# Scratch of the weight sums in a pool of its own, and the pools of the sums opened at once

## Chip, core and metric

The kernel runs on one core of one Trainium2 chip. The metric is the device time of one execution in microseconds (us), the median of several runs. The engines are TensorE (PE, its weight loads as PEld), VectorE (DVE), ScalarE (ACT), GpSimd (POOL) and SyncE (SP, which here only issues transfers). Each engine takes its instructions in the order of its own list and stops at the first one whose inputs are not there.

## What is computed

Sliding-window attention with eight global keys, then a two-layer network with a leaky ReLU. Four sequences of 768 positions, 8 heads of 64, give 3072 tokens of 512 numbers; the hidden width is 2048. The weights come as float64 and everything is to be right in float32, so each factor of the network is split into a high and a low part and each product takes three matmuls.

```python
scores = scale * np.matmul(q, k.transpose(0, 1, 3, 2))
keep = is_global | is_local
scores = np.where(keep, scores + bias, -1e9)
a = np.exp(scores - scores.max(-1, keepdims=True))
x = np.matmul(a / (a.sum(-1, keepdims=True) + 1e-09), v)   # per head, then tokens x 512
h = x @ w_in                                               # 512 -> 2048
return np.maximum(0.01 * h, h) @ w_out                     # 2048 -> 512
```

## The kernel before

Attention is cut into 48 units (24 blocks of 128 tokens, two halves of the heads). The work of unit t is spread over three events: event t forms its scores on PE, adds the bias and takes the row minimum on DVE (L224), takes the exponentials on ACT (L237), and scales them by the reciprocal of their sum (L258, L259, then L268 on DVE or L266 on ACT). From unit 14 on the probabilities `pr` are turned on DVE in blocks of 32 (L283) and sent by SP through memory, out as `via` (L248) and back as `pt_d` in four transfers (L250). Event t+2 multiplies them with the values (`attn_v`, L351) and ACT copies the result `x` (L357).

The network goes over the tokens in chunks: two chunks of three blocks, then nine of two. The first two chunks (the middle stage) work with one sixteenth of the hidden width at a time (`ffn1`, `ffn2`, helper lines L990 to L1012), beside the conversion of the weights. Its last outputs are held in three tiles `kept` of the pool `ev` and added to by DVE (L452). The nine chunks of the last stage work in 72 steps s, eight per chunk. Step s has one pair p of hidden blocks:

- `hidden_pair(s)`: 24 matmuls (L496) into one PSUM bank, `ps_h` for even s, `ps_p` for odd s.
- `gates(s)`: ACT copies the bank (L507), DVE applies the leaky ReLU (L509) and, where the pair is done with seven products in place of eight, four sums of its blocks (L512), ACT rounds to the high part `gh` (L516), DVE takes the rest `gl` (L518).
- `out_pair(s - 2)`: 12 matmuls with eight products, 21 with seven, over `gh` and `gl` (L548), two steps later.

So `gates` has two steps of PE time before its result is needed. Seven products stand in for eight because sums of blocks of the output weights `wout` are formed once, pair by pair. This is the work of `prepare(p, part)`: four parts for a pair, each three additions on DVE into two scratch tiles `wk` (L528), one rounding on ACT into `h` (L665) and one subtraction on DVE into `l` (L528); part 3 writes back into `wout`. In what follows, each such DVE instruction is called a sum instruction. The parts are handed to `gates` by the table `sums_at`: two parts a step at s = 2 to 7 (pairs 7, 6, 5, 4), then one a step at s = 8 to 23 (pair 3, the last part of pairs 7 to 4, then pairs 2 and 1).

The scratch tiles come from the pool `ev`, which has three buffers. The same three buffers hold `kept` before, and the output rows `part` and the tile `u` of `results` (L627) at the end of each chunk, from where SP sends them out (L460, L647). A tile that takes a buffer over waits until its last user is done, a transfer among them.

At s = 0 the pools of the middle stage are closed (`later`) and the pools `a` (gh, gl) and `w` (the sums h, l) are opened in their room.

PE's instructions are in the order of the program. Until the second chunk is through, those of ACT and DVE are too (`pin`); after that a scheduler orders ACT, DVE and SP by what each instruction waits for, and it may move an instruction ahead of others as soon as its inputs and its buffer allow.

Of the kernel before, what the change touches and what calls it, by code (L numbers as in the profile page):

```python
# [10 lines left out]
F32 = mybir.dt.float32  # L11
F32R = mybir.dt.float32r
# [6 lines left out]
P = 128  # L19
# [33 lines left out]
def fast_path(ctx, tc, qp, kp, vp, wi, wo, nvec, nmall, out, B, H, S):  # L53
# [10 lines left out]
    GT = P * PAIR  # L64
    NP = NF // 2
# [57 lines left out]
    def pin(ins):  # L123

        if pinned[0]:
            tc.keep_in_program_order(ins)
# [152 lines left out]
    def turn(u):  # L279

        pr = units[u].pop("pr")
        p = blocks(u, pr).rearrange("p c j x -> p (c j x)")
        pin(nc.vector.transpose(out=p, in_=p))  # L283
        move(u, pr)
# [90 lines left out]
    def event(t, conv=()):  # L375

        now, mid, old = t < NUNIT, t - 1 in units, t - 2 in units
        if t < LEAD + 2:

            av = (ps_lead if t % 2 else ps_x).tile([P, 2, 512], F32, tag="ps_av", name="ps_sc")  # L380
            scores(t, av)
            if mid:
                transposes(t - 1)
            if old:
                ov = ps_lead.tile([P, 2, 512], F32, tag="ps_ov", name="ps_ov")
                attn_v(t - 2, ov)
        else:

            ov = av = ps_x.tile([P, 2, 512], F32, tag="ps_av", name="ps_av")
            attn_v(t - 2, ov)  # L390
            if now:
                scores(t, av)
            if mid:
                transposes(t - 1)
            keep_x(t - 2, ov)
        if t + 2 < NUNIT:
            load_qk(t + 2)
        if t < NUNIT:
            load_v(t)
        if t < STAGES - 3:  # L400
            load_piece(t + 2)
        ends = due[:]
        due.clear()
        if ends:
            ends[0]()
        scale, shift, low = conversion(conv[0]) if conv else [lambda: None] * 3
        scale()
        if now:
            biased(t, av)
            exps(t)  # L410
        if ends:
            ends[1]()
        shift()
        if now:
            sums(t)
        low()
        if mid:
            keep_pt(t - 1)
        if old and t < LEAD + 2:
            keep_x(t - 2, ov)  # L420
        if old:
            split_x(t - 2)
# [39 lines left out]
    NS = (NCHUNK - STD) * NP  # L462
    pair = {}
    sides = {}

    def order_of(c):

        n = SEVEN[c - STD]
        return list(range(NP - n)) + list(range(NP - 1, NP - 1 - n, -1))

    def at(s):

        c = STD + s // NP
        return c, order_of(c)[s % NP]
# [3 lines left out]
    def fetch(s):  # L478

        if s >= NS:  # L480
            return
        p = at(s)[1]
        streamed[s] = ring.tile([P, 2, NK, P], F32R, name="ring")
        nc.scalar.dma_start(out=streamed[s].rearrange("p a k x -> p (a k x)").bitcast(F32), in_=wd[p])
# [15 lines left out]
    def gates(s, sums=()):  # L500

        c, p = at(s)
        ps = pair[s]
        n = 8 if fast(c, p) else 4
        t = late["t"].tile([P, 8, P], F32, name="t")
        g = t[:, :4].rearrange("p a b -> p (a b)")
        pin(nc.scalar.copy(out=g, in_=ps))  # L507
        fetch(s + RING)
        pin(nc.vector.scalar_tensor_tensor(out=g, in0=g, scalar=0.01, in1=g, op0=ALU.mult, op1=ALU.max))  # L509
        if n == 8:  # L510
            for o, x, y, op in ((4, 2, 0, ALU.add), (6, 1, 0, ALU.subtract), (5, 4, 1, ALU.subtract), (7, 3, 5, ALU.subtract)):
                pin(nc.vector.tensor_tensor(out=t[:, o], in0=t[:, x], in1=t[:, y], op=op))  # L512
        a0 = n // 8
        gh = late["a"].tile([P, 7, P], F32R, name="gh")
        gl = late["a"].tile([P, 7, P], F32R, name="gl")
        pin(nc.scalar.copy(out=gh[:, :n - a0], in_=t[:, a0:n]))  # L516
        rest = [prepare(p, part) for p, part in sums]
        pin(nc.vector.tensor_tensor(out=gl[:, :n - a0], in0=t[:, a0:n], in1=gh[:, :n - a0].bitcast(F32), op=ALU.subtract))  # L518
        for low in rest:
            low()  # L520
        pair[s] = gh, gl, a0

    def fast(c, p):

        return p >= NP - SEVEN[c - STD]

    def add(o, x, y, op=ALU.add):
        pin(nc.vector.tensor_tensor(out=o, in0=x, in1=y, op=op))  # L528
# [4 lines left out]
    def block(f, n):  # L533
        return tuple(wout[:, f, y, n * GT:(n + 1) * GT] for y in range(2))
# [114 lines left out]
    def prepare(p, part):  # L649

        e, o = 2 * p, 2 * p + 1
        first = p == NP - 1
        if part == 0:
            h = late["w"].tile([P, (4 if first else 3) * GT], F32R, tag=f"h{p}", name=f"h{p}")
            l = late["w"].tile([P, 3 * GT], F32R, tag=f"l{p}", name=f"l{p}")
            sides[p] = h, l
        h, l = sides[p]
        x, y = (late["ev"].tile([P, 2, GT], F32, tag="ev", name="wk")[:, n] for n in range(2))
        t1, t3, t2 = ((h[:, i * GT:(i + 1) * GT], l[:, j * GT:(j + 1) * GT]) for j, i in ((0, 0), (2, 3 if first else 2), (1, 1)))
        (ah, al), (bh, bl), (dh, dl) = ((block(e, 1), block(e, 0), t1), (block(o, 1), block(e, 1), t3), (block(o, 1), t1, t2),  # L660
                                        (block(o, 0), t2, block(e, 1)))[part]
        add(x, ah.bitcast(F32), al.bitcast(F32))
        add(y, bh.bitcast(F32), bl.bitcast(F32))
        add(x, x, y, ALU.subtract)
        pin(nc.scalar.copy(out=dh, in_=x))  # L665
        if first and part == 0:
            pin(nc.vector.memset(y, 0.0))
            pin(nc.scalar.copy(out=h[:, 2 * GT:3 * GT], in_=y))
        return lambda: add(dl, x, dh.bitcast(F32), ALU.subtract)
# [24 lines left out]
    late = {}  # L694
    for j in range(len(order)):
# [24 lines left out]
        if j >= half + NF:  # L720
            f = 2 * (j - half - NF) + 1
# [15 lines left out]
    for s in range(NS):  # L737
        pinned[0] = s == 0
        for t in ev_pair.get(s, ()):
            event(t)  # L740
        hidden_pair(s)
        if s == 0:
            ffn2(len(order) - 1)
            pinned[0] = False
            later.close()
            late["ev"] = rows_
            for name, n in (("a", 2), ("w", 1)):
                late[name] = ctx.enter_context(tc.tile_pool(name=name, bufs=n))
            nc.gpsimd.memset(late["w"].tile([P, 16], F32, tag="gap", name="gap"), 0.0)
        gates(s, sums_at.get(s, ()))  # L750
        for t in ev_pair.get(s, ()):
            if s and t < NUNIT:
                turn(t)
        if s >= 2:
            out_pair(s - 2)
        if s == NS - 4:
            band_holds()
        if s == NS - 2:
            all_hold()
# [318 lines left out]
```

## Time and profile before

| | us |
|---|---|
| median of three runs | 645.76 |
| lowest and highest | 643.36, 648.06 |
| the profiled execution | 645.19 |
| its span | 643.3 |
| PE busy in the span | 613.8 |
| DVE busy | 458.8 |
| ACT busy | 345.5 |
| POOL busy | 90.5 |
| first matmul of step 0 of the last stage | at 198.8 |

The times in the table are of the whole execution; the span is what the profiler saw from the first instruction to the last, and 1.9 us lie around it. All places below are given in us from the start of the span. In a row of the timeline the columns are start, duration, engine, line, operation, output <- inputs, count, and in brackets the idle time of that engine just before, with what ended it. In a list of waits the numbers are total, count and longest.

### The profile page before, as it was taken

The numbers are of one execution on the slowest core, as the hardware profiler recorded it, in microseconds if no ns is written. First come the engines' busy times: TensorE is split into PE (matmuls) and PEld (weight loads), VectorE is DVE, ScalarE is ACT, GpSimd is POOL, SyncE is SP. The second block draws the span as 40 slices with busy tenths as digits, with TensorE's granted clock in tenths as the row PEclk, the third lists the DMA queues.
The fourth block names the chain that finished last, engine by engine and source line by source line (L and its number), as shares of the span: only waits on it lengthen the run. The fifth ranks groups of instructions, "written<-read, shape, count | busy, mean of one in ns | idle before, by whom it ended". The sixth has DMA issues, their size and how long they took to land.

```text
span 643.3 us, 16794 instructions
## 1 busy us (share of the span) xinstructions
PE 613.8 (95%) x6537; PEld 565.7 (88%) x6537; DVE 458.8 (71%) x1286; ACT 345.5 (54%) x900; POOL 90.5 (14%) x148
## 2 busy tenths in 40 slices
PE   4769999999999999999989999999999999999995
PEld 3558889999888888899989999999999999999994
DVE  5979988887656995886696766765765765844653
ACT  5877855554544566455355665564565565532321
POOL 3345710000111001011011120110100100110000
PEclk9789999999999999999999999999999999999998
DMA  8786744430646767665755676765775774733321
GB/s 286 232 305 202 227 164 164 163 131 34 205 150 192 224 207 220 216 195 187 234 165 183 228 248 199 253 196 164 238 239 172 240 228 146 230 102 99 131 67 38
DMA packets 63336, 120.72 MB, mean 188 GB/s; under 512 B 8976, under 2 KB 28432, under 8 KB 63248
## 3 DMA queue, kind: packets, MB, share of 16 engines
q1 hardware_dynamic: 52880, 82.34, 40.2%
q10 hardware_dynamic: 10368, 37.23, 17.5%
q8 instruction: 53, 0.87, 0.6%
q14 instruction: 35, 0.29, 0.1%
HBM read 96.21 MB, written 23.33 MB: 186 GB/s over the span
## 4 chain that ended last, share of the span: by engine, by line
PE 84%; DVE 7%; DMA 4%; ACT 2%; POOL 1%; issue 1%; SPq 0%; DVEq 0%; ACTq 0%; POOLq 0%
PE ps_m L548 20%; PE ps_p L496 15%; PE ps_h L496 15%; PE ps_q L548 7%; PE ps_av L351 5%; PE ps_av L210 3%; PE ps_h L990 3%; PE ps_o L1010 3%; PE ps_o L1011 3%; PE ps_o L1012 3%; PE ps_h L992 3%; PE ps_h L991 3%; DMA vr<-in_vp_dram 1%; DMA kr<-in_kp_dram 1%; DVE pr L224 1%
## 5 line engine op out<-in xcount | busy, mean ns | idle before, releaser
L516 ACT CAST gh<-t 128x896 fp32r<-128x896 f32 (+1 forms) x72 | 61.8, 858 | 98.3 <-DVE t L512 63.1
L518 DVE TENSOR_TENSOR gl<-t,gh 128x896 fp32r<-128x896 f32 (+1 forms) x72 | 70.8, 983 | 47.5 <-ACT gh L516 47.4
L237 ACT ACTIVATE pr<-pr,nmall 128x192 f32<-128x192 f32 (+1 forms) x192 | 83.3, 436 | 29.1 <-DVE nmall L224 28.4
L49 POOL TENSOR_SCALAR xh<-x 128x256 fp32r<-128x256 f32 x48 | 29.1, 606 | 435.4 <-ACT x L357 352.3
L548 PE MATMUL ps_m<-wout,gh 128*128 128x256 f32 (+1 forms) x394 | 86.0, 300 | 0.0
L509 DVE SCALAR_TENSOR_TENSOR t<-t 128x512 f32<-128x512 f32 x72 | 49.5, 688 | 30.5 <-ACT t L507 29.6
L548 PEld LDWEIGHTS ps_m<-wout,gh 128*128 128x128 f32 x394 | 61.2, 188 | 1.6
L548 PE MATMUL ps_m<-wout,gl 128*128 128x256 f32 (+1 forms) x197 | 59.1, 300 | 0.0
L496 PE MATMUL ps_p<-xh,win 128*128 128x256 f32 x288 | 58.2, 287 | 0.0
L496 PE MATMUL ps_h<-xh,win 128*128 128x256 f32 x288 | 56.8, 282 | 0.0
L496 PE MATMUL ps_h<-xh,ring 128*128 128x256 f32 x288 | 55.7, 278 | 0.0
L496 PE MATMUL ps_p<-xh,ring 128*128 128x256 f32 x288 | 55.2, 277 | 0.0
L512 DVE TENSOR_TENSOR t<-t 128x128 f32<-128x128 f32 x212 | 51.9, 284 | 2.7
L496 PEld LDWEIGHTS ps_p<-xh,win 128*128 128x128 f32 x288 | 46.3, 188 | 6.0 <-issue 5.0
L224 DVE CUSTOM_DVE_ANT_0 pr<-ps_av,nbw 128x192 f32<-128x192 f32 x136 | 40.3, 352 | 13.1 <-ACT x L357 13.1
L496 PEld LDWEIGHTS ps_h<-xh,win 128*128 128x128 f32 x288 | 46.5, 188 | 2.4 <-issue 2.2
L548 PE MATMUL ps_m<-h,gh 128*128 128x256 f32 (+1 forms) x159 | 46.2, 291 | 0.9 <-ACT gh L516 0.9
L496 PEld LDWEIGHTS ps_h<-xh,ring 128*128 128x128 f32 x288 | 46.4, 189 | 0.0
L548 PE MATMUL ps_m<-h,gl 128*128 128x256 f32 x159 | 44.5, 280 | 2.0 <-DVE gl L518 2.0
L496 PEld LDWEIGHTS ps_p<-xh,ring 128*128 128x128 f32 x288 | 46.1, 188 | 0.1
L266 ACT ACTIVATE pr<-pr,rs 128x192 f32<-128x192 f32 (+1 forms) x116 | 42.5, 438 | 3.8 <-DVE rs L259 3.4
L548 PE MATMUL ps_q<-wout,gh 128*128 128x256 f32 (+1 forms) x182 | 44.4, 325 | 0.0
(150 smaller groups left out, 1627.7 us busy)
## 6 DMA issues: line engine op xcount, KB each, us to landing
ring<-wd ACTq DMA_DIRECT2D x70, 512.0 KB, 3.5
via<-pr SPq DMA_DIRECT2D x30, 384.0 KB, 3.1
pt_d<-via SPq DMA_DIRECT2D x120, 96.0 KB, 3.4
kr<-in_kp_dram SPq DMA_DIRECT2D x40, 256.0 KB, 4.1
vr<-in_vp_dram SPq DMA_DIRECT2D x40, 256.0 KB, 3.5
wst<-in_wi_dram SPq DMA_DIRECT2D x16, 512.0 KB, 3.8
wst<-in_wo_dram SPq DMA_DIRECT2D x16, 512.0 KB, 3.8
qs<-in_qp_dram SPq DMA_DIRECT2D x24, 256.0 KB, 4.4
```

The costliest lines, as they stand in the source:

```text
L49: return eng.tensor_scalar(out=dst, in0=src, scalar1=1.0, scalar2=1.0, op0=ALU.mult, op1=ALU.mult)
L210: tc.keep_in_program_order(nc.tensor.matmul(own(u, av[qf, j, a * KW:(a + 1) * KW]), lhsT=q[rows, a, qf], rhs=keys(rows, a, f), start=True, ...
L224: pin(nc.vector.tensor_tensor_reduce(out=head(u, pr, a, j), in0=own(u, ps[:, j, a * KW:(a + 1) * KW]), in1=nb, scale=-0.125, scalar=3.0e38 ...
L237: pin(nc.scalar.activation(out=p, in_=p, func=AF.Exp, scale=-1.0, bias=nm[:, 2 * a + j:2 * a + j + 1], accum_out=sm[:, 2 * a + j:2 * a + j ...
L266: pin(nc.scalar.activation(out=p, in_=p, func=AF.Copy, scale=rs[:, n:n + 1]))
L351: tc.keep_in_program_order(nc.tensor.matmul(av[out, a, cols], lhsT=v[rows, t, j, :], rhs=near(rows, j, t, fs), start=(n == 0), stop=(n == ...
L496: tc.keep_in_program_order(nc.tensor.matmul(o, lhsT=w[:, y, k], rhs=x[:, k, :], start=(k + i == 0), stop=(k == NK - 1 and i == 2)))
L509: pin(nc.vector.scalar_tensor_tensor(out=g, in0=g, scalar=0.01, in1=g, op0=ALU.mult, op1=ALU.max))
L512: pin(nc.vector.tensor_tensor(out=t[:, o], in0=t[:, x], in1=t[:, y], op=op))
L516: pin(nc.scalar.copy(out=gh[:, :n - a0], in_=t[:, a0:n]))
L518: pin(nc.vector.tensor_tensor(out=gl[:, :n - a0], in0=t[:, a0:n], in1=gh[:, :n - a0].bitcast(F32), op=ALU.subtract))
L548: tc.keep_in_program_order(nc.tensor.matmul(to, lhsT=x[:, a], rhs=y, start=first and n == 0, stop=last and n == 2))
```

## The change

The scratch tiles of the sums get a pool `wk` with three buffers of the same size. It lies behind the pool `w`, at the addresses that the sums h1, l1 of the last pair had. The tiles h, l of pairs 7 to 2 are now all taken when `w` is opened; h1, l1 are taken when part (1, 0) is reached, at s = 20: there `wk` is closed, a pool `w1` is opened in its room, and the scratch of the four parts of pair 1 comes from `ev` again. The room overlaps neither the weights nor the tokens that the middle stage uses after its second chunk; what was there before are tokens of that chunk. The instructions themselves, their number and their shapes are the same.

```diff
     sides = {}
+    spare = ExitStack()
...
-        if part == 0:
-            h = late["w"].tile([P, (4 if first else 3) * GT], F32R, tag=f"h{p}", name=f"h{p}")
-            l = late["w"].tile([P, 3 * GT], F32R, tag=f"l{p}", name=f"l{p}")
-            sides[p] = h, l
+        if (p, part) == (1, 0):
+            spare.close()
+            late["w"] = ctx.enter_context(tc.tile_pool(name="w1", bufs=1))
+            late["wk"] = late["ev"]
+            sides[p] = tuple(late["w"].tile([P, 3 * GT], F32R, tag=f"{name}{p}", name=f"{name}{p}") for name in "hl")
         h, l = sides[p]
-        x, y = (late["ev"].tile([P, 2, GT], F32, tag="ev", name="wk")[:, n] for n in range(2))
+        x, y = (late["wk"].tile([P, 2, GT], F32, tag="ev", name="wk")[:, n] for n in range(2))
...
             nc.gpsimd.memset(late["w"].tile([P, 16], F32, tag="gap", name="gap"), 0.0)
+            for p in range(NP - 1, 1, -1):
+                sides[p] = tuple(late["w"].tile([P, n * GT], F32R, tag=f"{name}{p}", name=f"{name}{p}")
+                                 for name, n in (("h", 4 if p == NP - 1 else 3), ("l", 3)))
+            late["wk"] = spare.enter_context(tc.tile_pool(name="wk", bufs=3))
         gates(s, sums_at.get(s, ()))
```

With it the scheduler's order changes in three stretches: from the last steps of the middle stage to s = 5, around s = 8 to 12, and around s = 16 to 20. PE's order is the same. The rows below, at three places, are the program's instructions in the order in which they stand on one engine, without times; the line numbers of the changed kernel are higher by one to six. In a row stand line, operation, output <- inputs and shape.

DVE, in the kernel before, from the scaling of the unit of step 0 on:

```order
L258 TENSOR_SCALAR rs<-sm 128x4
L259 RECIPROCAL rs<-rs 128x4
L268 TENSOR_SCALAR pr<-pr,rs 128x2x96 x4
L509 SCALAR_TENSOR_TENSOR t<-t 128x512
L283 STREAM_TRANSPOSE pr<-pr 128x768
L452 TENSOR_TENSOR kept<-ps_o,kept 128x512 x3
L518 TENSOR_TENSOR gl<-t,gh 128x512
```

DVE, in the changed kernel, the same stretch:

```order
L258 TENSOR_SCALAR rs<-sm 128x4
L510 SCALAR_TENSOR_TENSOR t<-t 128x512
L529 TENSOR_TENSOR wk<-wk 128x256
L259 RECIPROCAL rs<-rs 128x4
L529 TENSOR_TENSOR l_2821<-wk,h_2820 128x256
L529 TENSOR_TENSOR wk<-wout 128x256
L268 TENSOR_SCALAR pr<-pr,rs 128x2x96 x4
L529 TENSOR_TENSOR wk<-wout 128x256
L529 TENSOR_TENSOR l_2821<-wk,h_2820 128x256
L519 TENSOR_TENSOR gl<-t,gh 128x512
L283 STREAM_TRANSPOSE pr<-pr 128x768
L452 TENSOR_TENSOR kept<-ps_o,kept 128x512 x3
```

Five sum instructions now stand between the first and the turning of the probabilities, and the step's own `gl` has moved ahead of the turning. Twelve more stand before this stretch, between the last leaky ReLU of the middle stage and the bias of the unit of step 0, where none stood; here they are, again on DVE in the changed kernel:

```order
L1001 SCALAR_TENSOR_TENSOR t<-t 128x384
L529 TENSOR_TENSOR l_2819<-wk,h_2818 128x256
L529 TENSOR_TENSOR wk<-wout 128x256 x2
L1007 TENSOR_TENSOR gl<-t,gh 128x384
L529 TENSOR_TENSOR wk<-wk 128x256
L529 TENSOR_TENSOR wk<-h_2818,l_2819 128x256
L529 TENSOR_TENSOR l_2819<-wk,h_2818 128x256
L529 TENSOR_TENSOR wk<-wk 128x256
L529 TENSOR_TENSOR wk<-wout 128x256 x2
L529 TENSOR_TENSOR l_2819<-wk,h_2818 128x256
L529 TENSOR_TENSOR wk<-wk 128x256
L529 TENSOR_TENSOR wk<-wout 128x256
```

Between the bias and the row `rs<-sm` above stand five more, so 22 in all from the leaky ReLU to the turning; before there were none, and the first sum instruction came after the bias of the next unit.

SP, in the kernel before, the transfers around the one of the same unit (`via`, first row):

```order
L248 DMA via<-pr 128x768
L460 DMA out_dram<-kept 128x512
L190 DMA vr<-in_vp_dram 128x512
L460 DMA out_dram<-kept 128x512 x2
L250 DMA pt_d<-via 32x4x192 x4
L178 DMA kr<-in_kp_dram 128x512
L175 DMA qs<-in_qp_dram 128x512
L248 DMA via<-pr 128x768
L250 DMA pt_d<-via 32x4x192 x4
```

SP, in the changed kernel, where that `via` is the fourth row:

```order
L190 DMA vr<-in_vp_dram 128x512
L178 DMA kr<-in_kp_dram 128x512
L175 DMA qs<-in_qp_dram 128x512
L248 DMA via<-pr 128x768
L460 DMA out_dram<-kept 128x512 x3
L250 DMA pt_d<-via 32x4x192 x4
L248 DMA via<-pr 128x768
L190 DMA vr<-in_vp_dram 128x512
L178 DMA kr<-in_kp_dram 128x512
L250 DMA pt_d<-via 32x4x192 x4
```

The loads `vr`, `kr`, `qs` of later units have moved ahead of `via`, and all three rows of `kept` now stand between it and its `pt_d`.

The third place is DVE around the `gl` that PE uses at s = 21 (last row of each). In the kernel before:

```order
L528 TENSOR_TENSOR wk<-wout 128x256 x2
L283 STREAM_TRANSPOSE pr<-pr 128x768
L512 TENSOR_TENSOR t<-t 128x128
L528 TENSOR_TENSOR wk<-wk 128x256
L512 TENSOR_TENSOR t<-t 128x128
L509 SCALAR_TENSOR_TENSOR t<-t 128x512
L528 TENSOR_TENSOR wk<-h_4570,l_4571 128x256
L528 TENSOR_TENSOR l_4571<-wk,h_4570 128x256
L512 TENSOR_TENSOR t<-t 128x128 x2
L528 TENSOR_TENSOR wk<-wk 128x256
L518 TENSOR_TENSOR gl<-t,gh 128x896
```

In the changed kernel:

```order
L529 TENSOR_TENSOR wk<-wout 128x256
L529 TENSOR_TENSOR l_4578<-wk,h_4577 128x256
L513 TENSOR_TENSOR t<-t 128x128 x2
L259 RECIPROCAL rs<-rs 128x4
L529 TENSOR_TENSOR l_4578<-wk,h_4577 128x256
L513 TENSOR_TENSOR t<-t 128x128
L529 TENSOR_TENSOR wk<-h_4577,l_4578 128x256
L513 TENSOR_TENSOR t<-t 128x128
L529 TENSOR_TENSOR wk<-wk 128x256
L283 STREAM_TRANSPOSE pr<-pr 128x768
L519 TENSOR_TENSOR gl<-t,gh 128x896
```

The leaky ReLU and two block sums of the next step have moved behind this `gl`; between the `gl` before it and this one stand 11 sum instructions in place of 15.

## The prediction

> **What bounds the kernel.** I read the page's shares and its chain first, then who waits for whom on PE, on DVE, and then the timeline at the places of those waits.
>
> ```profile
> PE 613.8 (95%) x6537; PEld 565.7 (88%) x6537; DVE 458.8 (71%) x1286; ACT 345.5 (54%) x900; POOL 90.5 (14%) x148
> PE 84%; DVE 7%; DMA 4%; ACT 2%; POOL 1%; issue 1%; SPq 0%; DVEq 0%; ACTq 0%; POOLq 0%
> ```
>
> PE is busy for 613.8 of 643.3 us, so a faster DVE gains only what PE idles for it. The change can touch PE's idle time in the last stage alone. The waits of PE there are these two rows, and the waits of DVE for the shared buffers the two behind them:
>
> ```profile
> PE ps_m L548 <- DVE gl L518: 2.0, 2, 1.4
> PE ps_m L548 <- ACT gh L516: 0.9, 1, 0.9
> ...
> DVE wk L528 <- DMA out_dram<-part: 7.0, 3, 3.1
> DVE wk L528 <- DMA out_dram<-kept: 1.6, 1, 1.6
> ```
>
> DVE loses 8.6 us to transfers that still read the buffers its scratch wants, but PE loses only 2.9 us to `gh` and `gl` in the whole stage. Of these 2.32 lie at one place, s = 21, and the rest near the end, past the sums. So 2.3 us is the most that this change can win:
>
> ```profile
> 318.16 0.42 DVE L528 TENSOR_TENSOR wk<-h,l 128x256 f32<-128x256 f32 x1 [3.11 <-DMA out_dram<-part]
> ...
> 320.78 0.57 DVE L528 TENSOR_TENSOR wk<-wout 128x256 f32<-128x256 f32 x1 [1.74 <-DMA out_dram<-part]
> 321.27 1.08 DVE L518 TENSOR_TENSOR gl<-t,gh 128x896 fp32r<-128x896 f32 x1
> ...
> 329.99 0.68 DVE L509 SCALAR_TENSOR_TENSOR t<-t 128x512 f32<-128x512 f32 x1
> 330.21 0.93 ACT L516 CAST gh<-t 128x896 fp32r<-128x896 f32 x1
> 332.00 1.08 DVE L518 TENSOR_TENSOR gl<-t,gh 128x896 fp32r<-128x896 f32 x1
> 331.20 0.38 PE L548 MATMUL ps_m<-h,gh 128*128 128x256 f32 x1 [0.88 <-ACT gh L516]
> 333.13 0.39 PE L548 MATMUL ps_m<-h,gl 128*128 128x256 f32 x1 [1.44 <-DVE gl L518]
> ```
>
> DVE stands for 3.11 and 1.74 us, then has more queued than it can do before PE wants the `gl` of s = 19, and PE idles 0.88 + 1.44 = 2.32 us.
>
> **The edits, and what each costs.** The new pool, the early taking of h and l and the later taking of h1, l1 add no instruction; all three cost only by the order that follows. No row shows the freed room itself. What the first `wk` waits for is the last matmul of the second chunk, which the leaky ReLU next to it on DVE waits for as well, so I take 0 for it (from below no gain is possible either, nothing else stood there).
>
> *At s = 18 to 21.* The scratch of pair 1 comes from `ev` again, and the changed order has it just there: its second and third scratch tile wait for the same two transfers of `part` as the two rows above. So the 3.11 and 1.74 us stay. What changes is the queue between the `gl` at 321.27 and that at 332.00. Before, it holds 15 sum instructions and, ahead of the second `gl`, the next step's leaky ReLU and two block sums; in the changed order 11 and none of the next step. DVE's rhythm for sum instructions is:
>
> ```profile
> 228.64 0.75 DVE L528 TENSOR_TENSOR wk<-wout 128x256 f32<-128x256 f32 x2
> 229.31 0.42 DVE L528 TENSOR_TENSOR wk<-wk 128x256 f32<-128x256 f32 x1
> ```
>
> Two take 0.67 us from start to start, 0.335 each. Four fewer are 1.34 us, the ReLU is 0.6 and the two block sums 0.4: `gl` could start 2.3 us earlier. Its chain still goes through ACT, where `gh` (0.93 us) now stands behind two roundings and four scalings of the unit, and I cannot resolve that to better than a microsecond. The bounds are 0 and 2.32 us; I take a gain of 1.3, past the middle because DVE's share alone would give nearly all.
>
> *At the start of the last stage.* Here is the work that the hoisted sums pass, and the path of the probabilities of the unit of step 0:
>
> ```profile
> 195.89 0.56 DVE L995 SCALAR_TENSOR_TENSOR t<-t 128x384 f32<-128x384 f32 x1 [1.01 <-ACT t L994]
> 197.03 0.56 DVE L1001 TENSOR_TENSOR gl<-t,gh 128x384 fp32r<-128x384 f32 x1 [0.58 <-ACT gh L1000]
> 199.41 0.36 DVE L224 CUSTOM_DVE_ANT_0 pr<-ps_av,nbw 128x192 f32<-128x192 f32 x1 [1.82 <-ACT x L357]
> ...
> 201.71 0.17 DVE L258 TENSOR_SCALAR rs<-sm 128x4 f32<-128x4 f32 x1 [1.10 <-ACT pr L237]
> ...
> 203.66 0.97 DVE L283 STREAM_TRANSPOSE pr<-pr 128x768 f32<-128x768 f32 x1
> 204.55 1.85 DVE L452 TENSOR_TENSOR kept<-ps_o,kept 128x512 f32<-128x512 f32 x3
> 206.32 0.67 DVE L518 TENSOR_TENSOR gl<-t,gh 128x512 fp32r<-128x512 f32 x1
> 206.91 0.35 DVE L224 CUSTOM_DVE_ANT_0 pr<-ps_av,nbw 128x192 f32<-128x192 f32 x1
> ...
> 204.65 0.33 SPq L248 DMA_DIRECT2D via<-pr  x1
> ...
> 207.76 1.89 SPq L250 DMA_DIRECT2D pt_d<-via  x4
> 209.74 0.40 SPq L178 DMA_DIRECT2D kr<-in_kp_dram  x1
> ...
> 213.68 1.09 PE L351 MATMUL ps_av<-pt_d,vr 64*64 64x128 f32 x24
> ...
> via<-pr SPq DMA_DIRECT2D x1, 384.0 KB, 2.7
> pt_d<-via SPq DMA_DIRECT2D x1, 96.0 KB, 3.5
> ```
>
> The last two rows are of the list of transfers, for this `via` and the last of its `pt_d`; they end with the us from issue to landing. From the ReLU at 195.89 to the turning at 203.66 are 7.77 us, of which DVE idles 0.58 + 1.82 + 1.10 = 3.50 and works 4.27. The 22 sum instructions that now stand in between are 22 x 0.335 = 7.37 us, and the `gl` moved ahead of the turning 0.59 (206.32 to 206.91). If they fill the idle time wholly, the turning starts at 195.89 + 4.27 + 7.37 + 0.59 = 208.1, later by 4.5. From there the path is as before: `via` 0.99 us later at 209.1, `pt_d` 3.11 us after it at 212.2, the last of its four 1.27 us later (209.03 before) at 213.5, landed 3.5 us on at 217.0. Before, that was 212.5, and PE's `attn_v` of step 3 began at 213.68: a margin of 1.1 us. Now PE waits from 213.7 to 217.0, 3.3 us, with all its later work queued behind. The moved `vr`, `kr`, `qs` wait for the unit of step 1 on PE, which was past it before its bias began on DVE at 206.91, so they don't hold `via`. The three rows of `kept` need DVE's additions, 0.6 each after the turning, so the last is issued near 212, just when `via` has landed; I cost them at nothing. Bounds: DVE cannot pass 22 instructions in less than I counted, but `via` and `pt_d` may be quicker or slower, by these rows:
>
> ```profile
> DMA to landing us min/median/max: 1.9/3.2/6.9
> DMA to landing us min/median/max: 1.9/3.3/6.2
> ```
>
> The first is `via`, the second `pt_d`. At the fastest the wait is 3.3 - 0.8 - 1.6 = 0.9 us, with `via` at its slowest 3.3 + 4.2 = 7.5. I take 3.3, the transfers of this very unit.
>
> *What else moves.* The work that the other moved instructions feed stands here in the chain of work:
>
> ```profile
> 210.84 0.62 PE L548 MATMUL ps_m<-wout,gh 128*128 128x512 f32 x2
> ...
> 226.95 0.83 PE ps_av L351 x32
> ...
> 245.11 0.83 PE ps_av L351 x32
> ```
>
> ACT's roundings into h7, h6 and h5 now stand ahead of the `x` copy of step 0 and the bank copies of steps 0 and 1 (three of 0.4 us, then one that waits for DVE until about 211). The `ps_p` copy of step 1 then ends near 212 and its bank is wanted again by step 3, behind the `attn_v` at 213.68: hidden. The first `out_pair` at 210.84 wants `gl` of step 0 (near 208) and the first `kept` addition (near 209.7): hidden, by 1 us. The units of steps 1 and 3 are turned later too, but are wanted two events on, at 226.95 and 245.11: hidden. Around s = 8 to 12 the third of DVE's waits for `part` goes, 7.0 - 3.11 - 1.74 = 2.15 us, and the list of PE's waits shows nobody behind it: 0.
>
> **Sum.** 645.19 + 3.3 - 1.3 = 647.2 us, against the profiled execution, which lies 0.6 below the median of the three runs.
>
> **Rivals.** (1) *Slower: PE's clock falls in the gap.* The new gap of 3.3 us would be the longest of all. Here is what the gaps at the start did, the longest being 2.39, and the short ones at 331:
>
> ```profile
> 14.19 1.56 PE L210 MATMUL ps_sc<-kr,qs 64*64 64x192 f32 x16 [2.39 <-DMA kr<-in_kp_dram]
> ...
> 20.00:25.00 5.00, 3.54 (x104) 2.81 (x108) 4.93 (x21) 4.80 (x15) 2.79 (x6) 0.60 0.80 265
> 25.00:30.00 5.00, 4.29 (x138) 3.67 (x134) 4.59 (x15) 4.50 (x16) 2.49 (x4) 0.72 0.84 290
> 30.00:40.00 10.00, 7.03 (x222) 5.95 (x219) 8.30 (x30) 8.43 (x28) 4.06 (x6) 0.83 0.94 331
> ...
> 328.00:332.00 4.00, 2.82 (x23) 2.41 (x21) 4.00 (x13) 1.27 (x3) 0.00 (x0) 1.00 0.46 179
> ```
>
> The last figures of a row are granted clock, DMA share and GB/s. After a row of gaps the clock was 0.60, 0.72 and 0.83 for 20 us, a loss of 2.0 + 1.4 + 1.7 = 5.1 us of PE; after the gap at 331 it was 1.00. A fall as deep would end at 652.3, a third as deep at 648.9; it needs a gap much beyond 2.4 us, which mine is. For it speaks the length, against it that PE works without pause before and after. [...]
>
> (2) *Slower: `via` lands late*, since three outputs of `kept` start right behind it on the same queue. At the slowest landing of the trace the wait is 7.5 us: 651.4. Against it, before they started right behind it as well and it took 2.7.
>
> (3) *Faster: PE doesn't wait at step 3*, because DVE does not come to the hoisted sums as densely or PE reaches step 3 later than I think; then only the gain counts, 643.9, at most 642.9. It needs the turning to start before 204.8, that is, 10 fewer sum instructions ahead of it than the order shows.
>
> (4) *Nothing: the change doesn't do what it says.* The same two waits for `part` stay, the gain comes to nothing and the wait at step 3 is short: 645 to 646.
>
> **Chances.** My forecast 0.55, (1) 0.10, (2) 0.08, (3) 0.15, (4) 0.12. The forecast's own range is 645.5 (wait 2.0, gain 1.7) to 649.0 (wait 4.5, gain 0.7). The whole range reaches to 643.0, the best of (3), and to 651.5, the end of (2), and leaves out the deep fall of (1). About 1% is what a measurement of this kernel can tell from no change; from 645.19 that is 638.7 to 651.6. Faster than that PE's idle time does not allow: 0.02. Slower needs (1) deep or (2) with no gain: 0.08. Within: 0.90.
>
> **What would show it.** In the changed profile PE should have a wait of about 3.3 us before L351 at step 3, for the transfer of `pt_d`; the turning L283 of that unit should start near 208 in place of 203.7, with sum instructions from 196 on; the wait of DVE for `part` should be down to two, near 318 and 321 plus the shift; and PE's wait at s = 21 should be near 1 us. No wait at step 3 makes the prediction wrong in its main term; a clock below 1.00 right after it means (1); a `via` of over 5 us means (2).

## The result and the profile after

| | before | after |
|---|---|---|
| median of 22 runs each, us | 645.58 | 650.46 |
| lowest and highest | 642.15, 648.28 | 647.10, 657.24 |
| ratio | | 1.0078, 95% interval 1.0061 to 1.0096 |
| the profiled execution | 645.19 | 653.33 |
| its span | 643.3 | 651.6 |

The changed kernel is 0.8% slower, 4.9 us at the medians; the ratio leaves out its slowest run, 657.24 us. The time lies in the whole range stated and the change within the 1% that was called none. But it lies above the 645.5 to 649.0 of the forecast itself, and the loss is more than twice the 2.0 us that the sum came to. The profiled execution is 2.9 us above the median of its kernel, so a second one of the same kernel was taken later (`after2`, 648.95 us); where the two differ, both are told.

First PE in the last stage as a whole. The two rows are from the view by stretches, for the kernel before and then for the changed one: stretch, its length, then busy time and count of PE, PEld, DVE, ACT and POOL, granted clock, DMA share, GB/s.

```profile
198.80:643.30 444.50, 434.43 (x4476) 408.39 (x4472) 304.25 (x868) 227.15 (x584) 45.23 (x64) 0.99 0.59 188
```

```profile
199.23:651.60 452.37, 438.36 (x4476) 411.94 (x4472) 302.09 (x858) 226.60 (x581) 44.23 (x64) 0.98 0.58 185
```

The stage begins 0.43 us later and takes 7.87 us more. PE idles 452.37 - 438.36 = 14.01 us in place of 10.07, 3.94 more, and the same 4476 matmuls take 3.93 us more. So half of the loss is waiting, and the other half is matmuls that run slower. The idle time counts the end of the stage too, in which PE has no work left: from the start of the last matmul to the end of the span it is 7.5 us before and 6.2 here, so the waits within the stage have grown by more than 3.94. The list of PE's waits of the changed kernel has the waiting (total, count, longest):

```profile
PE ps_av L351 <- ACT gh L517: 4.8, 1, 4.8
PE ps_p L497 <- DMA ring<-wd: 2.0, 1, 2.0
PE ps_m L549 <- DVE gl L519: 1.2, 2, 0.6
```

The first is the wait at step 3 that the prediction spoke of, 4.8 us in place of its 3.3. The wait for `gl` at s = 21 has shrunk from 2.32 to 0.6 (the other 0.5 lies at the end, as before). The wait for `ring` is new. The name in the first row misleads, which the timeline shows:

```profile
196.81 0.42 DVE L529 TENSOR_TENSOR l<-wk,h 128x256 fp32r<-128x256 f32 x1
...
209.00 0.96 DVE L283 STREAM_TRANSPOSE pr<-pr 128x768 f32<-128x768 f32 x1
209.99 0.33 SPq L248 DMA_DIRECT2D via<-pr  x1
210.72 1.37 SPq L460 DMA_DIRECT2D out_dram<-kept  x3
212.10 0.33 ACTq L485 DMA_DIRECT2D ring<-wd  x1
212.78 1.79 SPq L250 DMA_DIRECT2D pt_d<-via  x4
218.98 2.02 PE L351 MATMUL ps_av<-pt_d,vr 64*64 64x128 f32 x23 [4.79 <-ACT gh L517]
```

The sums start at 196.81, the turning at 209.00, `pt_d` is issued from 212.78, and PE's `attn_v` starts at 218.98 after 4.79 us of standing still. No `gh` is among its inputs; what came last was `pt_d`. Its landing is in the view of that tile, us from issue to landing:

```profile
DMA to landing us min/median/max: 5.4/5.5/5.7
```

Here is what follows that gap, in stretches of 2 us, the clock being the third figure from the end:

```profile
216.00:218.00 2.00, 0.00 (x0) 0.00 (x0) 2.00 (x6) 1.40 (x5) 0.00 (x0) 1.00 1.13 258
218.00:220.00 2.00, 0.88 (x6) 0.55 (x10) 2.00 (x6) 0.95 (x3) 0.00 (x0) 0.54 0.79 229
220.00:222.00 2.00, 2.00 (x43) 1.90 (x42) 1.94 (x5) 0.41 (x1) 0.00 (x0) 0.50 0.55 209
222.00:224.00 2.00, 2.00 (x14) 1.47 (x8) 0.89 (x7) 1.16 (x5) 0.75 (x2) 0.50 0.63 143
224.00:226.00 2.00, 2.00 (x15) 2.00 (x15) 2.00 (x10) 1.38 (x7) 0.39 (x1) 0.76 0.87 235
226.00:228.00 2.00, 2.00 (x13) 1.76 (x13) 1.03 (x5) 0.89 (x2) 0.00 (x0) 1.00 0.36 103
```

The clock is at half from 218.16 (0.54 is 92% of a stretch at half) to 224.96 (0.76 is 48%), for 6.8 us. PE works from 218.98 on, so 5.98 us of matmuls do the work of 2.99 if all run at half speed: the first rival came on top of the forecast. The next `attn_v` starts here (the kernel before, then the changed one):

```profile
226.88 0.90 PE L351 MATMUL ps_av<-pt_d,vr 64*64 64x128 f32 x32
```

```profile
234.84 0.90 PE L351 MATMUL ps_av<-pt_d,vr 64*64 64x128 f32 x32
```

From the `attn_v` of step 3 that is 13.20 us before and 15.86 here, with no wait in either. So the fall cost 2.7 us, or 3.1 against the 12.78 of the run with the sums held back, below. The wait for `ring` has a tail of the same kind, shorter:

```profile
350.00:352.00 2.00, 1.55 (x10) 1.55 (x11) 1.97 (x5) 0.24 (x1) 0.00 (x0) 0.82 0.99 335
352.00:354.00 2.00, 2.00 (x11) 2.00 (x11) 0.91 (x4) 1.37 (x2) 0.00 (x0) 0.50 0.61 167
354.00:356.00 2.00, 2.00 (x16) 1.89 (x14) 1.97 (x5) 0.06 (x1) 0.00 (x0) 0.83 0.80 249
```

By the same reading that is half clock from 351.28 to 354.68, 3.4 us, a loss of up to 1.7. What leads up to the wait is seen in the order of time of DVE, ACT and PE (rows picked from the timeline):

```profile
326.36 0.42 DVE L529 TENSOR_TENSOR wk<-wout 128x256 f32<-128x256 f32 x1 [3.35 <-DMA out_dram<-part]
329.01 0.54 DVE L529 TENSOR_TENSOR wk<-wout 128x256 f32<-128x256 f32 x1 [1.76 <-DMA out_dram<-part]
...
343.68 0.46 ACT L237 ACTIVATE pr<-pr,nmall 128x192 f32<-128x192 f32 x1 [1.17 <-DVE nmall L224]
344.65 0.33 ACTq L485 DMA_DIRECT2D ring<-wd  x1
...
345.01 0.44 ACT L237 ACTIVATE pr<-pr,nmall 128x192 f32<-128x192 f32 x1
...
350.45 0.39 PE L497 MATMUL ps_p<-xh,ring 128*128 128x256 f32 x1 [2.00 <-DMA ring<-wd]
```

DVE's two waits for `part` stand where they were forecast, 5.1 us in all. DVE is late for the rest of the step, the exponentials on ACT wait for DVE, the fetch of the ring tile for s = 23 stands behind them in ACT's list (its issue, at 344.65, was 0.36 us ahead of the last of them, at 345.01), and PE wants that tile 3.8 us after its issue (348.45) while it lands after 5.8. What PE gained at s = 21 it gives back two steps later.

### The profile page after: what moved, and what is told of

It reads as the page before. It is cut to its first block, busy times and chain, and to the rows that moved or that the text cites. A ratio compares the mean times of both kernels' runs of the same rounds, so it can differ in the third digit from the quotient of the medians.

```text
span 651.6 us, 16792 instructions
## 1 busy us (share of the span) xinstructions
PE 617.0 (95%) x6537; PEld 568.7 (87%) x6537; DVE 459.9 (71%) x1286; ACT 346.1 (53%) x900; POOL 89.2 (14%) x148
## 4 chain that ended last, share of the span: by engine, by line
PE 79%; DMA 7%; DVE 6%; ACT 3%; issue 2%; SPq 1%; POOL 1%; ACTq 0%; DVEq 0%; POOLq 0%
PE ps_m L549 19%; PE ps_p L497 15%; PE ps_h L497 14%; PE ps_q L549 6%; PE ps_av L351 5%; PE ps_av L210 3%; PE ps_h L996 3%; PE ps_o L1016 3%; PE ps_o L1017 3%; PE ps_o L1018 3%; PE ps_h L998 3%; PE ps_h L997 3%; DMA vr<-in_vp_dram 3%; DMA kr<-in_kp_dram 2%; ACT pr L237 1%
## 5 line engine op out<-in xcount | busy, mean ns | idle before, releaser
L549 PE MATMUL ps_m<-l,gh 128*128 128x256 f32 x159 | 44.5, 280 | 0.0
```

The costliest lines, as they stand in the source:

```text
L549: tc.keep_in_program_order(nc.tensor.matmul(to, lhsT=x[:, a], rhs=y, start=first and n == 0, stop=last and n == 2))
```

## Experiments

The theory: the hoisted sums make the turning late, the late turning makes PE wait for `pt_d`, and the gap makes the clock fall. The rivals to it: the freed room or the other order later in the stage costs the time; the fall of the clock is chance; the long landing of `pt_d` has another cause than its neighbours. Waits and clocks come from one profiled execution of each kernel. Ratios stand against the kernel before, run on the same chip.

### The changed kernel with the sums held back

```diff
             late["wk"] = spare.enter_context(tc.tile_pool(name="wk", bufs=3))
+            for n in range(3):
+                nc.vector.tensor_copy(out=late["wk"].tile([P, 16], F32, tag="ev", name="held"), in_=kept[n][:, :16])
```

> The changed kernel with three tiny DVE copies (128x16) that write into the three wk buffers from the three kept tiles, so that no weight sum can start before the last additions to kept; the pool, its room and the early taking of h and l stay. Theory (the sums that moved ahead of the turning L283 of step 0's unit cost the time): the turning is back at 203.5 to 205, PE's wait before L351 at step 3 is under 0.5 us, the clock from 216 to 226 is 1.00, and the time is 643.5 to 645.5 us, that is 5 to 7 below the changed kernel. Rival (the room or the other order later in the stage costs it): no wait at step 3, yet the time stays at 649 to 651.

645.28 us, ratio 1.0007 (0.9986 to 1.0028): as the kernel before. The turning stands at 203.90, there is no wait at step 3, and the clock behind it is full:

```profile
203.90 0.97 DVE L283 STREAM_TRANSPOSE pr<-pr 128x768 f32<-128x768 f32 x1
...
216.00:226.00 10.00, 10.00 (x69) 9.14 (x68) 9.97 (x34) 6.90 (x21) 1.55 (x2) 1.00 0.70 210
...
PE ps_p L497 <- DMA ring<-wd: 2.8, 1, 2.8
```

The room and the early taking are all still there, so the 4.9 us belong to the sums that moved ahead of the turning. The last row says why nothing is gained either: at s = 21 PE waits no more, but at s = 23 it waits 2.8 us for `ring` in this execution, with 6.8 us at half clock behind it, the same turn as in the changed kernel. (DVE waited only 3.3 us for `part` here; the fetch itself took 6.7 us to land, so the reason isn't wholly the same.)

### The early taking alone

```diff
-            late["wk"] = spare.enter_context(tc.tile_pool(name="wk", bufs=3))
+            late["wk"] = late["ev"]
```

> The changed kernel with the scratch taken from the pool ev, as before; what stays is that the sums h and l of pairs 7 to 2 are taken at once and those of pair 1 in a second pool. Theory (the scratch's own buffers move the sums, the early taking does nothing): no sum ahead of the turning, no wait at step 3, the time within 1 us of the kernel before. Rival (the early taking itself moves work): the turning later than 206 and a wait of over 1 us at step 3.

645.65 us, ratio 1.0014 (0.9993 to 1.0035). The turning is at 205.38 with a stage that begins 1.7 us later, so it isn't late, and PE has no wait for `pt_d`. Taking h and l early moves nothing that costs. (PE's wait for `gl` at s = 21 is 0.8 us in this execution, in place of 2.32: it too varies with small moves.)

### A late turning in the kernel before

```diff
+        if u == 18:
+            for _ in range(13):
+                pin(copy_exact(nc.vector, p[:, :256], p[:, :256]))
```

This stands ahead of the turning L283 (L286 here); two more kernels have 6 and 9 in place of 13.

> The kernel before, with 13 multiplications by one (128x256, in place, on DVE) ahead of the turning L283 of step 0's unit; nothing else changes. 13 x 0.335 = 4.4 us of delay against a margin of 1.1. Theory (a late turning alone is the price): a wait of about 3.3 us before L351 at step 3 if pt_d lands 3.5 us after its issue as in the kernel before, about 5 if it lands after 5.5 as in the changed one; time 3.3 above the kernel before without a fall of the clock, about 6 above with one from about 218 on. Rival (the loss comes from elsewhere in the changed order): a wait under 1 us, time within 1 us of the kernel before.

> The kernel before with 6 multiplications by one (128x256, in place, on DVE) ahead of the turning L283 of step 0's unit, and by them its gl too. Their rows in the run with 13 took 0.31 us each. The turning should start near 206.6, 3 us late, and PE wait about 2 us before L351 at step 3. Theory (the clock falls only behind a gap of well over 2.4 us): clock 1.00 from 216 to 226, time 2 us above the kernel before. Rival (any gap above the ones at hand makes it fall): clock near 0.7 there, time 5 above.

> The same with 9 multiplications; by its order half of the next unit's bias stands ahead of the turning too, so the turning should start near 208.3, as late as in the changed kernel, with none of its weight sums moved. [...] Rival (the changed kernel's wait came from its transfers and sums beside the path): a wait of under 2.5 us and a clock of 1.00.

The waits of PE before `attn_v` of step 3, for 13, 9 and 6, and the stretch 216 to 226 with its clock, in the same order:

```profile
220.27 1.89 PE L354 MATMUL ps_av<-pt_d,vr 64*64 64x128 f32 x23 [5.20 <-DMA pt_d<-via]
```

```profile
218.67 1.78 PE L354 MATMUL ps_av<-pt_d,vr 64*64 64x128 f32 x23 [5.80 <-ACT h L671]
```

```profile
216.42 0.40 PE L354 MATMUL ps_av<-pt_d,vr 64*64 64x128 f32 x2 [2.28 <-DVE t L512]
218.22 0.73 PE L354 MATMUL ps_av<-pt_d,vr 64*64 64x128 f32 x22 [1.40 <-DMA pt_d<-via]
```

```profile
216.00:226.00 10.00, 5.73 (x59) 4.69 (x60) 8.11 (x21) 1.95 (x5) 0.00 (x0) 0.66 0.53 173
```

```profile
216.00:226.00 10.00, 7.33 (x74) 6.36 (x75) 9.92 (x33) 4.71 (x16) 1.89 (x2) 0.66 0.53 154
```

```profile
216.00:226.00 10.00, 8.18 (x81) 7.12 (x82) 9.50 (x31) 5.60 (x18) 1.26 (x2) 0.83 0.64 188
```

The times are 653.55 (ratio 1.0128, 1.0086 to 1.0171), 650.66 (1.0109, 1.0071 to 1.0147) and 651.73 us (1.0097, 1.0063 to 1.0130). A late turning (207.25 with 9, 206.53 with 6, against 203.66), with the sums where they were, is enough for a loss of this size: the run with 9 has such a wait, 5.80 us, and the clock (0.66) and the time of the changed kernel. It doesn't come by quite the same path, though. `via` landed in 5.7, 4.3 and 4.0 us here (13, 9 and 6) in place of the 2.7 of both kernels, which adds 1.3 to 3.0 us; with 13 `pt_d` itself landed in 2.6, so the wait of about 5 us that was expected there came for another reason.

With 9 the wait is 1.0 us longer than the changed kernel's 4.79. With 6 the expectation missed: the wait is 3.7 us in two pieces in place of 2, and the clock falls all the same, for half as long (3.4 us); a turning under 3 us late already costs some 6 us. About 5 of these lie at step 3 in the profile. The rest lies at s = 21, where PE's waits of 0.55 and 1.43 us had 3.4 us at half clock behind them. The run with 13 had such a stretch there too, while nearly the same waits left the clock at 1.00 in the kernel before.

### The gap filled with matmuls

```diff
+            if t == 20:
+                for _ in range(36):
+                    tc.keep_in_program_order(nc.tensor.matmul(av[:, 0, :256], lhsT=win[0][:, 0, 0], rhs=xt[STD][0][:, 0, :],
+                                                              start=True, stop=True))
             attn_v(t - 2, ov)
```

> The changed kernel with 36 more matmuls (128x256, into a bank whose content is overwritten behind them, output unchanged) ahead of attn_v of step 3, that is, in PE's gap of 4.8 us. At 0.11 us each they fill about 4 us. Theory (the clock falls for six us because PE stood still for long): the wait left is about 1 us, the clock stays 1.00 from 216 to 226, and the time is 2 to 3 us below the changed kernel. Rival (the clock falls for another reason, or not as a rule): the time is the same as the changed kernel's or up to 1 us above, the clock from 218 to 224 is about 0.5 all the same.

```profile
214.40 4.27 PE L392 MATMUL ps_av<-xh,win 128*128 128x256 f32 x36
219.10 0.40 PE L351 MATMUL ps_av<-pt_d,vr 64*64 64x128 f32 x2 [0.43 <-DMA pt_d<-via]
219.88 0.73 PE L351 MATMUL ps_av<-pt_d,vr 64*64 64x128 f32 x22 [0.37 <-DMA pt_d<-via]
...
216.00:226.00 10.00, 9.19 (x104) 8.23 (x103) 10.00 (x29) 4.65 (x14) 1.48 (x1) 1.00 0.58 172
```

`pt_d` comes as late as before, but PE was idle for only 0.43 and 0.37 us, and the clock stays at 1.00 where it was 0.66: the standing still is the cause of the fall. The time is 649.37 us, ratio 1.0098 (1.0073 to 1.0124). That is 1.1 us below the changed kernel's median and 1.4 below that of its second series, not the 2 to 3 expected, and the intervals overlap: the fall is shown, its price in the median isn't resolved. The profiles show it more closely. From the start of the `attn_v` before that of step 3 to the start of the one after it PE takes 28.1 us here, 30.6 and 30.4 in the two executions of the changed kernel and 23.1 before: without the fall 2.3 to 2.5 us are saved. Later this run loses 1.5 us to a wait for `ring`, which the second execution of the changed kernel, below, does not have.

### The changed kernel once more

> The changed kernel once more, unaltered, for a second execution with a profile. Theory (three losses belong to the changed order and come back in each execution): a wait of 4 to 5.5 us before L351 at step 3, a granted clock of about 0.5 for some six us after it, and a wait of 1 to 3 us for a ring fetch near s = 23; the time 649 to 652 us. Rival (the fall of the clock or the ring wait was chance in one execution): the wait at step 3 is there, the clock from 216 to 226 is above 0.9, or no wait for ring over 0.7 us.

```profile
PE ps_av L351 <- DVE wk L529: 4.4, 1, 4.4
PE ps_m L549 <- DVE gl L519: 0.5, 1, 0.5
...
216.00:226.00 10.00, 7.83 (x74) 6.81 (x75) 8.64 (x28) 5.42 (x18) 1.14 (x2) 0.66 0.71 206
```

650.78 us, ratio 1.0095 (1.0071 to 1.0120). The wait at step 3 and the clock at half are there again; the wait for `ring` is not, against the expectation, nor any at s = 21. In this execution DVE waited 2.5 us for `part` in place of 5.1, and was not late. So the first two losses come with the order in both executions. The third goes with how fast the outputs leave: in the profiles with this order, waits for `part` of 5.1 to 3.9 us come with waits for `ring` of 2.3 to 1.4. The mean granted clock over the runs of this series is 0.9858, that of the kernel before beside it 0.9897; one stretch of 6.8 us at half in 648 would be 0.0052. That would fit a fall in most executions, but doesn't show it: the profiled run with 9 multiplications has such a stretch and a mean of 0.992, so the mean moves with other stretches as well.

### What makes `pt_d` slow

Two kernels take one neighbour away each: the first sends the rows of `kept` out by 64 of 512 columns and leaves the rest of these rows unwritten, the second holds the ring fetch of step 3 until `pt_d` has landed.

```diff
-            nc.sync.dma_start(out=out[r0:r0 + P, :], in_=ob)
+            nc.sync.dma_start(out=out[r0:r0 + P, :64], in_=ob[:, :64])
```

```diff
+        if s == 3:
+            nc.gpsimd.tensor_copy(out=streamed[s][:, 0, 0, :4], in_=units[18]["pt"][:, :4])
-        nc.scalar.dma_start(out=streamed[s].rearrange("p a k x -> p (a k x)").bitcast(F32), in_=wd[p])
+        (nc.gpsimd if s == 3 else nc.scalar).dma_start(out=streamed[s].rearrange("p a k x -> p (a k x)").bitcast(F32), in_=wd[p])
```

> The changed kernel with the last rows of the first two chunks sent out by their first 64 of 512 columns (the rest of these rows stays unwritten), so that the three outputs between via and pt_d move 96 KB in place of 768. Theory (the ring fetch that is issued just ahead of pt_d is what makes its landing 5.5 us instead of 3.5): pt_d still lands 5 us or more after its issue, the wait at step 3 stays at 4 to 5 us. Rival (the outputs are in its way): pt_d lands in 3.5 to 4 us and the wait is 2 to 3 us.

> The changed kernel with the ring fetch of step 3 held until pt_d of step 0's unit has landed (a tiny GpSimd copy from pt_d into the ring tile ahead of it, the fetch issued by GpSimd). Theory (that fetch delays pt_d by 2 us): pt_d lands in 3.5 to 4 us, the wait at step 3 falls to about 3 us, as the prediction had it, and the ring tile then comes up to 1.5 us late. Rival (pt_d is slow by the outputs or by itself): it still takes over 5 us, the wait at step 3 stays at 4.4 to 4.8, and the ring comes 3 us late or more on top.

The landing of `pt_d` in the first, then in the second of them:

```profile
DMA to landing us min/median/max: 4.1/4.2/4.7
```

```profile
DMA to landing us min/median/max: 2.5/2.7/2.9
```

Against 5.5 in the changed kernel, the outputs account for some 1.3 us and the fetch for some 2.8: both are in the way, the fetch more, and neither theory had it whole. (The two figures don't add up to a landing: together they would leave 1.4 us, less than any seen here.) With the fetch held the wait at step 3 falls from 4.8 to 2.2 us, but the ring tile then comes 4.2 us late, not the 1.5 expected at most, and the clock falls to 0.50 there; the time is 653.79 us (1.0110, 1.0070 to 1.0150). With the outputs cut the wait is 3.29 + 1.09 us, and the one time taken is 653.98. Over the profiles with all these transfers whole, the landing goes with the time of the nearest ring fetch, though these kernels differ in more than that:

| kernel | ring fetch issued, against the first `pt_d` | `pt_d` landing, median us |
|---|---|---|
| changed | 0.7 us ahead | 5.5 |
| changed, second execution | 0.7 ahead | 5.2 |
| before, 9 multiplications | 1.2 ahead | 5.5 |
| changed, gap filled | 0.7 ahead | 5.3 |
| before, 6 multiplications | 1.6 behind, one more 2.0 ahead | 4.3 |
| before, 13 multiplications | 5.5 ahead | 2.6 |
| before | 2.2 behind | 3.6 |
| changed, sums held | 2.1 behind | 3.6 |
| changed, early taking alone | 2.2 behind | 3.6 |

### The ring fetch on another queue

Three kernels move the fetch from ACT's list to GpSimd's. The first has the sums held back and all fetches moved, the second the same with the fetches moved from step 20 on, the third is the kernel before with that second edit alone.

```diff
-        nc.scalar.dma_start(out=streamed[s].rearrange("p a k x -> p (a k x)").bitcast(F32), in_=wd[p])
+        (nc.gpsimd if s >= 20 else nc.scalar).dma_start(out=streamed[s].rearrange("p a k x -> p (a k x)").bitcast(F32), in_=wd[p])
```

> The changed kernel with the sums held back by the three tiny copies, as in the run before, and with the ring fetches issued by GpSimd in place of ScalarE. Theory (the gain at s = 21 is lost again at s = 23, where the ring fetch stands too late in ScalarE's order): no wait for ring over 0.5 us, none at step 3, waits for gl of at most 1 us in all, time 642 to 643.5 us, that is 0.3% below the kernel before. Rival (the ring's fetch is late because the transfer is slow, whoever issues it): a ring wait of 1.5 us or more stays, time as the kernel before.

> The changed kernel with the sums held back by the three tiny copies, and the ring fetches issued by GpSimd from step 20 on, by ScalarE before that. Theory (the held order has nothing to lose at step 3, the gain at s = 21 is lost at s = 23 where ScalarE issues the ring fetch late, and GpSimd's early fetch at step 3 was what delayed pt_d in the run with all fetches there): no wait at step 3, none for ring over 0.5 us, waits for gl under 1 us in all; time 642 to 643.5, that is 1.5 to 2.5 us below the kernel before. Rival (the lag of DVE behind PE around s = 21 is only shifted): a wait of 1.5 us or more for gl, gh or ring stays between 300 and 350, time within 1 us of the kernel before.

> The kernel before with the ring fetches issued by GpSimd from step 20 on, by ScalarE before that: the fetch's move without the changed order. Theory (what made the held version with this split 0.6% faster is the gain at s = 21 of the changed order, kept because the fetch no longer gives it back; the kernel before has no ring wait that the split could remove): waits of 1.5 to 2.5 us for gl and gh near s = 21 stay, the time is within 1.5 us of the kernel before. Rival (the split alone is the gain): those waits fall below 1 us and the time is 2 us or more below.

With all fetches moved the time is 644.77 us, ratio 0.9999 (0.9981 to 1.0018), not the 642 to 643.5 expected. The ring wait is gone, as the theory said, but a new one stands at step 3, because one fetch now goes out 0.5 us behind the first `pt_d`:

```profile
217.14 0.73 PE L351 MATMUL ps_av<-pt_d,vr 64*64 64x128 f32 x22 [2.34 <-DMA pt_d<-via]
```

With the fetches moved from step 20 on only, PE's waits in the whole last stage are one row:

```profile
PE ps_m L549 <- DVE gl L519: 0.5, 1, 0.5
```

641.70 us, ratio 0.9938 (0.9912 to 0.9964): faster than both kernels, by 0.6% against the one before. The third run then took part of the credit from the change. The kernel before with the split alone has these waits:

```profile
PE ps_av L351 <- DMA pt_d<-via: 0.7, 1, 0.7
PE ps_m L548 <- DVE gl L518: 0.5, 1, 0.5
```

The wait at s = 21 is gone there too, against the theory, though the time, 642.75 us, ratio 0.9971 (0.9946 to 0.9996), is still inside the 1.5 us that it gave. So moving the fetch is worth about 0.3% by itself, and whether the pool of its own adds to it isn't settled: the two intervals overlap. The move also lets the scheduler order ACT and DVE otherwise, and which of the two does away with the wait at s = 21 wasn't tried. Nor is it certain that the move does it at all. In the profiles of the kernel before and of those made from it, PE's wait at s = 21 follows DVE's wait for `part` just ahead: 2.3 us behind 4.8 in the kernel before, 2.4, 2.0 and 0.9 behind 4.0, 4.1 and 3.1 with 13, 6 and 9 multiplications, none behind 2.8 in this run. How far the move shortens the wait for `part`, and how far that varies by itself, no run here separates.

## Why the prediction was right, and where it was off

**Right in the mechanism and in the class.** The sums from 196 on (196.81), the turning near 208 (209.00, and 208.40 in the second execution), the two waits for `part` (3.35 and 1.76 us), a wait at step 3 for `pt_d`, and a smaller wait at s = 21 (0.6) are all in the profile. Holding the sums back took the loss away, and a late turning without them brought a loss of its size back, in part by a slower `via`. In the changed kernel `via` landed in 2.7 us as taken, so the second rival fell; the third and fourth fell with the wait. That the whole range held the time is partly luck: its upper end is that of the second rival, which did not come, and two terms that the sum had too small or not at all, the landing and the clock, filled the room.

**The turning.** Forecast 4.5 us late; less the 0.51 us by which PE itself reached step 3 later, it is 209.00 - 0.51 - 203.66 = 4.83. Close.

**The mis-sized term: `pt_d` "landed 3.5 us on".** It measured 5.5. With it 4.5 - 1.1 + 2.0 = 5.4 would have been forecast, against 4.8 and 4.4. The step behind it is "I cost them at nothing": the three outputs of `kept` were only weighed for `via`, and the ring fetch not at all, while delaying the path by 4.5 us put it just behind the fetch that had come after it. The bound of 7.5 covers the wait, but it was worked out from a slow `via`, not from a slow `pt_d`.

**The missing term: the clock.** The sum had none, and the first rival had a chance of 0.10 and a price of 1.7 to 5.1 us. It came in both executions of the changed kernel, at some 3 us in each. The prediction called its condition, "a gap much beyond 2.4 us", met by its own gap of 3.3, and still gave it 0.10 and nothing in the sum. The condition was the author's estimate, and no run shows it: 2.00 us were enough at `ring`, and the profile of the kernel before, which the prediction read in slices of 5 and 10 us, shows the same in slices of 2. Here are a gap at the start and what follows it, and one slice from further on:

```profile
20.18 0.94 PE L305 MATMUL ps_tr<-dg,pr 64*64 64x64 f32 x48 [2.07 <-POOL dg L275]
...
20.00:22.00 2.00, 1.82 (x72) 1.76 (x76) 2.00 (x8) 2.00 (x7) 1.23 (x3) 0.74 0.67 172
22.00:24.00 2.00, 1.04 (x16) 0.37 (x8) 1.93 (x8) 1.80 (x7) 0.64 (x1) 0.50 1.01 376
24.00:26.00 2.00, 1.68 (x56) 1.68 (x60) 2.00 (x10) 2.00 (x7) 1.37 (x3) 0.50 0.69 243
26.00:28.00 2.00, 2.00 (x48) 1.68 (x40) 1.86 (x5) 1.50 (x6) 0.50 (x1) 0.55 0.83 246
...
34.00:36.00 2.00, 0.97 (x20) 1.00 (x24) 1.93 (x6) 1.27 (x6) 0.02 (x1) 0.66 0.97 381
```

The 0.60, 0.72 and 0.83 are no fall over 20 us but two falls to half: 6.8 us from 20.96 on, behind a gap of 2.07 with another of 1.28 within, and 3.4 us from 34.6 on, about a gap of 1.30. The longest gap, 2.39, has 1.00 behind it. So the prediction, which looked at the longest gap, missed what shorter ones do show: tails that cost up to 1.7 or 3.4 us of PE time could be read from the trace at hand, and the 5.1 us of a deep fall were the two added up. The experiments have tails of the same two lengths, 3.4 us (6 multiplications; `ring`) and 6.8 (step 3 of the changed kernel). A term that the trace at hand shows twice, behind gaps shorter than the forecast's 3.3 us, deserved more than 0.10.

**The gain.** Forecast 1.3, measured 1.7 (2.32 to 0.6) in the first execution, with DVE's waits for `part` nearly as long as before. The 2.3 of the second execution aren't all the order's, since DVE waited less for `part` there. But the gain was counted as final. In the first execution the next thing late was the ring tile of s = 23, 2.0 us of waiting and 1.7 of clock; the prediction looked at ACT for `gh` alone and not at the fetch in ACT's list.

**The sum as it came.** First execution: +4.8 wait, +3.0 clock, -1.7 gain, +2.0 and +1.7 at `ring`, +0.4 a later start, 10.2 in all against 8.3 measured between the spans. Of the 1.9 between, 1.3 lie behind the last matmul, where the end came sooner (6.2 in place of 7.5 us); that matmul starts 9.6 us later than before, which leaves 0.6 open. Second: +4.4, +3.0, -2.3, -0.2, 4.9 against 3.9.

## What to carry to other kernels

Giving scratch its own buffers took DVE's waits for transfers from 8.6 to 5.1 us here and let the scheduler hoist the work that had waited; ask what that work now stands in front of, and follow that thing through its transfers to the engine that sets the end. A transfer that is delayed is also moved next to other transfers (`pt_d` landed in 5.5 us here, in 3.6 before): take its landing from the neighbours at its new place, not from its old row. And a wait on the matrix engine may bring a tail at half clock (3.4 us behind 2.00, 6.8 behind 4.79 here): read the clock in slices shorter than the tail, and give the tail a chance and a price in the sum.

## What the runs showed of the hardware

A gap on PE could cost more than its length (4.79 us, and 2.7 us more behind it, in the changed kernel). Stretches at half clock within the kernels lasted 3.4 or 6.8 us. In the last stage they were 3.4 us behind single gaps of 2.00 and 2.30 us (`ring`, in the changed kernel and in the run with the outputs cut), and behind pairs of gaps with work between (2.28 and 1.40; 3.29 and 1.09; 0.55 and 1.43; 0.96 and 1.43). They were 6.8 us behind single gaps of 2.8 to 5.8, in six profiles. A single gap of 2.34 us (all fetches moved), one of 1.96 (the fetch of step 3 held) and the pair of 0.88 and 1.44 in the kernel before left the clock at 1.00, so near 2 us the length alone did not decide it here; no run shows what did. The median landing of the four transfers of 96 KB went from 2.6 to 5.5 us over the kernels, and from 5.5 to 4.2 or 2.7 with one neighbour, the outputs or the fetch, taken away. And a wait that ends with several inputs was put down to `gh`, `gl`, `wk`, `t` or `h` by the list of waits, in six profiles, where what PE still lacked were the transfers of `pt_d`.
